# Conv on eight small tiles from a shifted copy, eight output buffers and a regrouped start, in a Conv + low-rank mixer kernel

## The chip, the cores and the metric

The kernel runs on one core of one Trainium2 chip. The metric is the device time of one execution in microseconds (us). Before the change the median of 8 runs is 340.77 us (338.88 to 341.13). A core has a matrix engine (TensorE, in the profile PE for its matmuls and PEld for its weight loads), a vector engine (DVE), an activation engine (ACT), GpSimd (POOL) and SyncE (SP). The last two only start DMA transfers here, apart from some set-up work on POOL. Matmul results go to PSUM[...]; DVE or ACT must copy ("evacuate") them to SBUF.

## What is computed

```python
# x: [8, 4224, 192], weight: [8 heads, 7 taps], U: [4224, 32], V: [32, 4224]
w = softmax(weight, axis=-1)
y[b, s, head h] = sum over k of w[h, k] * x_pad[b, s + k, head h]   # causal, 6 zero rows ahead
h = (y.transpose(0, 2, 1) @ U @ V).transpose(0, 2, 1)
u = y + h
out = u + maximum(u @ w_ch1, 0) @ w_ch2          # w_ch1: [192, 768], w_ch2: [768, 192]
```

The first line of work is called Conv below, the second the low-rank sum, and the two matrix products of the last line W1 and W2.

## The kernel before

*Layout.* The sequence of a batch is cut into 66 blocks of 64 rows. An x tile has 128 partitions: the lower 64 hold blocks 0 to 31 with an empty block ahead, the upper 64 hold blocks 31 to 65, the first again as the halo. It is loaded from HBM in four parts (XP, L83) by POOL, which also turns f32 into bf16. x tiles come from a pool of three (xs, L46).

*Conv* (L297). One call does some heads of one batch. The weights are a band matrix per head. Each output of 64 rows takes two matmuls: one with the block itself, one with the block ahead of it (halo), accumulated in PSUM. Both have 64 input rows and 64 output rows[...]. For one head of batches 1 to 7 these are eight matmuls of 384 or 408 columns into two banks; row half r writes bank r. ACT evacuates one bank, DVE the other (L272, L274).

*Low-rank sum.* tt_mm (L334) multiplies the Conv result by U, 33 small matmuls (L340). tt_split (L350) splits it in a high and a low half, tt_sum (L393) adds four row groups, and tt_done copies the sum to SBUF (L390). h_group (L456, called "h" in the plan) then makes u for a group of eight 128-row tiles: small matmuls (L425), and DVE additions that write u (L447).

*The mixer.* SP transposes u by DMA (L466) into uT; w1 (L511) does 36 matmuls of 512 columns (L519), whose results ACT and DVE pass through a ReLU (L530, L532); w2 (L537) does 12 matmuls of 192 columns per two tiles (L543), DVE adds u (L551) into one of four output buffers (outs, L51), and SP stores it (L558). 33 groups in all.

*Order.* The program order of each engine is written out by hand. SLOTS (L571) lists, per slot, the groups for w1, the groups for w2, the Conv heads between them, and at which w2 piece other steps stand: h (with the transpose of that group), t (tt_mm and tt_split) and s (tt_sum). From slot 5 on a slot has three groups: w1 of three groups, then Conv, then 12 w2 pieces with the other steps between them. The x parts of a later batch are started by POOL, each held until a given block of w1 has run (LOADS, L607, and held, L611). DMAs of one queue are issued in program order, so a transfer that waits holds up those behind it.

*Start.* Batch 0 is loaded and convolved in three pieces (KP, L85; x_piece, L87). While the weights of the Conv are being built, PE runs matmuls on zeros (idle, L170): 60 of 128 columns, then three and two of 512 columns around the first piece. The first two groups get their transposes from PE (L477, L492).

Of the kernel before, what the change touches and what calls it, by code (L numbers as in the profile page):

```python
# [9 lines left out]
BF16 = mybir.dt.bfloat16  # L10
# [4 lines left out]
def kernel(  # L15
# [10 lines left out]
    nc = tc.nc  # L26
    P = nc.NUM_PARTITIONS
    B, S, D = x.shape
    H, KC = weight.shape
    GS = D // H  # L30
    R = moe_U.shape[1]
    M4 = moe_w_ch1.shape[1]
    NT = S // P
# [6 lines left out]
    HB = P // 2  # L40
    QB = 32
# [1 line left out]
    ctx.enter_context(tc.manual_schedule())  # L43

    cst = ctx.enter_context(tc.tile_pool(name="cst", bufs=1))
    xs = ctx.enter_context(tc.tile_pool(name="xs", bufs=3))  # L46
    ys = ctx.enter_context(tc.tile_pool(name="ys", bufs=3))
    us = ctx.enter_context(tc.tile_pool(name="us", bufs=7))
    uts = ctx.enter_context(tc.tile_pool(name="uts", bufs=5))
    rls = ctx.enter_context(tc.tile_pool(name="rls", bufs=3))  # L50
    outs = ctx.enter_context(tc.tile_pool(name="outs", bufs=4))  # L51
    sml = ctx.enter_context(tc.tile_pool(name="sml", bufs=2))
    psp = ctx.enter_context(tc.tile_pool(name="psp", bufs=8, space=bass.MemoryType.PSUM))

    def bank():
        return psp.tile([P, 512], F32, name="ps", tag="ps")
# [4 lines left out]
    xt = [None] * B  # L61
    yt = [None] * B
# [3 lines left out]
    NB0 = 32  # L66
    NB1 = S // HB - NB0
# [14 lines left out]

    XP = [(0, 1, 17), (0, 17, NB0 + 1), (1, 0, 18), (1, 18, NB1 + 1)]  # L83

    KP = [(0, 7), (7, 13), (13, NB1 // 2)]  # L85

    def x_piece(k):  # L87
        for r in range(2):
            k0, k1 = KP[k]
            k1 = min(k1, (NB0, NB1)[r] // 2)  # L90
            x_part(0, r, (1 - r if k == 0 else 2 * k0 + 1), 2 * k1 + 1)
# [25 lines left out]

    fp = cst.tile([P, P], I32, name="fp")
    nc.gpsimd.iota(fp[:], pattern=[[1, P]], base=P, channel_multiplier=-1)
    x_piece(1)  # L120

    efp = cst.tile([P, 4, P], I32, name="efp")
    nc.gpsimd.iota(efp[:], pattern=[[-1, 4], [1, P]], base=4 * P, channel_multiplier=-4)
# [8 lines left out]
    )  # L132
    nlast = NT * 32 - nfull * P
    nc.gpsimd.dma_start(out=Ur[0:nlast, nfull, :], in_=U4[nfull * P :, :])
    x_piece(2)


    V0_sb = cst.tile([32, 2 * GT * P], BF16, name="V0_sb")
# [31 lines left out]
    def idle(n, w):  # L170
        wps = bank()
        for _ in range(n):
            nc.tensor.matmul(  # L173
                out=wps[:, 0:w], lhsT=zz[:, 0:P], rhs=zz[:, 0:w], start=True, stop=True
            )
# [94 lines left out]
    def evac(eng, out, in_):  # L270
        if eng == "A":
            nc.scalar.activation(out=out, in_=in_, func=ACT.Copy)  # L272
        else:
            nc.vector.tensor_copy(out=out, in_=in_)  # L274
# [19 lines left out]
            )  # L294


    def conv(b, h0, nh, rs, engs, k0=0, k1=NT):  # L297

        if yt[b] is None:
            yt[b] = ys.tile([P, NT, D], BF16, name="y_sb")  # L300
        nk = {r: min(k1, (NB0, NB1)[r] // 2) - k0 for r in rs}
        pp = {r: bank() for r in rs}
        w = nh * GS
        for hh in range(nh):
            h = h0 + hh
            for halo in range(2):
                for r in rs:
                    for c in range(2):
                        st = 1 - halo + c + 2 * k0
                        nc.tensor.matmul(  # L310
                            out=pp[r][HB * c : HB * c + HB, 0 : nk[r] * w].rearrange(
                                "p (k a) -> p k a", a=w
                            )[:, :, hh * GS : hh * GS + GS],
                            lhsT=band[HB * r : HB * r + HB, h, HB * halo : HB * halo + HB],
                            rhs=xt[b][
                                HB * r : HB * r + HB,
                                st : st + 2 * nk[r] - 1 : 2,
                                h * GS : h * GS + GS,
                            ],
                            start=(halo == 0),  # L320
                            stop=(halo == 1),
                            tile_position=(HB * r, HB * c),
                        )
        for n, r in enumerate(rs):
            j0 = NB0 // 2 * r + k0
            evac(
                engs[n % len(engs)],
                yt[b][:, j0 : j0 + nk[r], h0 * GS : h0 * GS + w],
                pp[r][:, 0 : nk[r] * w].rearrange("p (k a) -> p k a", a=w),
            )  # L330
# [55 lines left out]
            )  # L386

    def tt_done(b, p):
        t = sml.tile([P, D], BF16, name="tt_sb")
        nc.vector.tensor_copy(out=t[:], in_=p[:, 0:D])  # L390
        ttb[b] = t

# [71 lines left out]
    def transp(g):  # L464
        uTt[g] = uts.tile([P, 4, 3, P], BF16, name="uT")
        nc.sync.dma_start_transpose(  # L466
            out=uTt[g][:].rearrange("p i c t -> p (i c) t"),
            in_=ut[g][:].rearrange("p i c f k -> p (i c f k)"),
        )
# [90 lines left out]
    def held(ins, after):  # L560
        tc.add_manual_dep(
            ins.ins,
            after.ins.name,
            mybir.DependencyInfo(mybir.DependencyClass.Sync, mybir.DependencyReason.DATA),
            reason="load held back",
        )
# [2 lines left out]


    SLOTS = [  # L571
        ([0], [], [], {}),
        ([1], [0], [], {0: ["h0"], 1: ["h3"]}),
        ([2], [1], [(1, 0, 8)], {0: ["h1"], 1: ["t1"], 3: ["s1"], 4: ["h4"]}),
        ([3], [2], [(2, 0, 4)], {1: ["h5"]}),
        (
            [4, 5],
            [3, 4, 5],
            [(2, 4, 8)],
            {1: ["t2", "h6"], 3: ["s2"], 4: ["h7"], 7: ["h8"], 10: ["h9"]},  # L580
        ),
    ]
    CONV = {
        5: [(3, 0, 8)],
        6: [(4, 0, 8)],
        7: [(5, 0, 4)],
        8: [(5, 4, 8), (6, 0, 3)],
        9: [(6, 3, 8), (7, 0, 2)],
        10: [(7, 2, 8)],
    }  # L590
    SUMS = {5: (3, 5), 6: (4, 10), 8: (5, 2), 9: (6, 6), 10: (7, 10)}
    nh = 10
    for k in range(5, 14):
        gs = list(range(3 * k - 9, 3 * k - 6))
        at = {}
        for p in (1, 5, 9) if k == 5 else (2, 6, 10):
            if nh < NG:
                at.setdefault(p, []).append(f"h{nh}")
                nh += 1
        if k in SUMS:  # L600
            b, p = SUMS[k]
            at.setdefault(p, []).insert(0, f"t{b}")
            at.setdefault(p + 2, []).insert(0, f"s{b}")
        SLOTS.append((gs, gs, CONV.get(k, []), at))
    assert nh == NG

    LOADS = {2: [(1, 5), (1, 5), (2, 2), (2, 5)]}  # L607
    for b, g in ((3, 4), (4, 6), (5, 9), (6, 12), (7, 15)):
        LOADS[b] = [(g, 1), (g, 4), (g + 1, 1), (g + 1, 4)]

    def held(ins, after):  # L611
        tc.add_manual_dep(
            ins.ins,
            after.ins.name,
            mybir.DependencyInfo(mybir.DependencyClass.Sync, mybir.DependencyReason.DATA),
            reason="load held back",
        )


    idle(3, 512)  # L620
    for h in range(0, H, 2):
        conv(0, h, 2, [0, 1], "AD", *KP[0])
    idle(2, 512)
    for h in range(0, H, 2):
        conv(0, h, 2, [0, 1], "AD", *KP[1])
    u_layout()
    yT = yT_part(0)
    jb = NB0 // 2
    rest = [(KP[2][0], jb), (jb + KP[2][0], NT)]
    ps0 = bank()  # L630
    U4_sb, tf = tt_first(
        ps0, list(range(KP[2][0])) + list(range(jb, jb + KP[2][0])), rest
    )
    for h in range(0, H, 4):
        conv(0, h, 4, [0, 1], "AD", *KP[2])
    nc.tensor.matmul(out=ps0[:, 0:D], lhsT=R4f[:], rhs=tf[:], start=True, stop=False)  # L636
    tt_more(ps0, U4_sb, rest)
    tt_done(0, ps0)
# [4 lines left out]
        x_part(1, *xp)  # L643

    def do(what):
        n = int(what[1:])
        if what[0] == "h":
            h_group(n)
            if n > 1:
                transp(n)  # L650
        elif what[0] == "t":
            tt_split(n, tt_mm(n, range(NT)))
        else:
            tt_sum(n)

    for gs1, gs2, convs, at in SLOTS:
        for g in gs1:
            ends = w1(g, RELU0 if g < 2 else RELU)
            for b, blocks in LOADS.items():
                for q, (gb, m) in enumerate(blocks):  # L660
                    if gb == g:
                        if q == 0:
                            x_tile(b)
                            x_zero(b, nc.gpsimd)
                        held(x_part(b, *XP[q]), ends[m])
            if g == 0:
                hT_part(1, yT_part(1), "AD")
                do("h2")
        n = sum(h1 - h0 for _, h0, h1 in convs)
        for b, h0, h1 in convs:  # L670
            for h in range(h0, h1):
                conv(b, h, 1, [0, 1], "AD" if n > 2 else "A")
        npc = 4 * len(gs2)
        for p in range(npc + 1):
            for what in at.get(p, []):
                do(what)
            if p < npc:
                g, k = gs2[p // 4], p % 4
                if g == NG - 1 and k == 3:
                    w2(g, 6, 1)  # L680
                    w2(g, 7, 1)
                else:
                    w2(g, 2 * k, 2)
# [30 lines left out]
```

## Time and profile before

| | |
|---|---|
| median of 8 runs | 340.77 us |
| the profiled execution | 340.99 us |
| its span | 339.2 us |
| mean granted PE clock | 0.993 |
| DMA traffic | 53.55 MB, mean 158 GB/s |
| DMA queue of SP | 38.18 MB, 45.2% of 16 engines |
| DMA queue of POOL | 14.73 MB, 37.4% |
| landing of a store of 192 KB, median | 2.8 us |
| landing of a part of x, median | 7.5 to 9.1 us |
| landing of a transpose, median | 4.0 us |

Busy time of an engine is the union of its instructions. Matmuls are pipelined and their ends are modelled, so PE can be busy and still not run at its peak; distances between the starts of two groups of matmuls are the safer measure. In lines of groups, "x133 | 70.1, 551" means 133 instructions, 70.1 us busy together, 551 ns each; behind the second bar stands the idle time of the engine just before them and what ended most of it. In timelines the columns are the start, the duration from the first to the last instruction of the merged group, engine, line and operation. In the chain of waits they are start, duration and instruction. A store's or a load's landing time is counted from its issue to the last byte.

### The profile page before, as it was taken

The numbers are of one execution on the slowest core, as the hardware profiler recorded it, in microseconds if no ns is written. First come the engines' busy times: TensorE is split into PE (matmuls) and PEld (weight loads), VectorE is DVE, ScalarE is ACT, GpSimd is POOL, SyncE is SP. The second block draws the span as 40 slices with busy tenths as digits, with TensorE's granted clock in tenths as the row PEclk, the third lists the DMA queues.
The fourth block names the chain that finished last, engine by engine and source line by source line (L and its number), as shares of the span: only waits on it lengthen the run. The fifth ranks groups of instructions, "written<-read, shape, count | busy, mean of one in ns | idle before, by whom it ended". The sixth has DMA issues, their size and how long they took to land.

```text
span 339.2 us, 9771 instructions
## 1 busy us (share of the span) xinstructions
PE 327.1 (96%) x4111; PEld 231.4 (68%) x4111; DVE 280.4 (83%) x571; ACT 160.4 (47%) x327; POOL 39.3 (12%) x65
## 2 busy tenths in 40 slices
PE   8789999999999999999999999999999998999995
PEld 7555675678557856965974884696587487487595
DVE  5736999988888888988898889889898887886863
ACT  1648446550492097059039308704912911922910
POOL 8660210120120040012012000000000000000000
PEclk9979999999999999999999999999999999999999
DMA  9999995699996999799799696069049238429135
GB/s 107 192 167 135 167 209 130 126 193 255 183 207 103 223 195 134 197 192 204 123 277 183 108 230 146 2 186 234 2 112 243 69 90 237 96 72 254 48 118 165
DMA packets 122941, 53.55 MB, mean 158 GB/s; under 512 B 87792, under 2 KB 122864, under 8 KB 122896
## 3 DMA queue, kind: packets, MB, share of 16 engines
q1 hardware_dynamic: 84672, 38.18, 45.2%
q0 software_dynamic: 38224, 14.73, 37.4%
q8 instruction: 32, 0.52, 0.6%
q14 instruction: 13, 0.11, 0.1%
HBM read 29.49 MB, written 25.95 MB: 163 GB/s over the span
## 4 chain that ended last, share of the span: by engine, by line
PE 77%; DVE 8%; DMA 8%; ACT 3%; issue 2%; POOL 1%; DVEq 0%; POOLq 0%
PE ps L519 35%; PE ps L543 30%; DMA out_dram<-out_sb 8%; PE ps L310 7%; DVE out_sb L551 3%; ACT rl_sb L530 2%; PE ps L340 2%; DVE u_sb L447 2%; PE ps L425 2%; DVE y_sb L274 1%; DVE pr L223 1%; DVE rl_sb L532 1%; POOL x_sb L78 1%; PE ps L173 0%; PE ps L636 0%
## 5 line engine op out<-in xcount | busy, mean ns | idle before, releaser
L530 ACT ACTIVATE rl_sb<-ps 128x512 bf16<-128x512 f32 x235 | 126.0, 604 | 108.5 <-PE ps L519 87.0
L543 PE MATMUL ps<-W_sb,rl_sb 128*128 128x192 bf16 x1584 | 139.1, 246 | 1.8 <-DVE out_sb L551 1.7
L543 PEld LDWEIGHTS <-rl_sb 128*128 128x128 bf16 x1584 | 128.9, 98 | 10.7 <-issue 10.4
L519 PE MATMUL ps<-uT,W_sb 64*128 64x512 bf16 x1188 | 133.5, 376 | 1.7 <-DVE uT L274 0.8
L532 DVE TENSOR_SCALAR rl_sb<-ps 128x512 bf16<-128x512 f32 x161 | 104.0, 688 | 15.3 <-PE ps L519 14.9
L519 PEld LDWEIGHTS <-W_sb 64*128 64x128 bf16 x1188 | 61.4, 94 | 69.5 <-issue 7.2
L551 DVE TENSOR_TENSOR out_sb<-ps,u_sb 128x384 f32<-128x384 f32 (+1 forms) x133 | 70.1, 551 | 25.9 <-DMA out_dram<-out_sb 12.8
L447 DVE TENSOR_TENSOR u_sb<-y_sb,ps 128x192 bf16<-128x192 bf16 (+1 forms) x168 | 66.2, 461 | 0.0
L78 POOL DMA_DIRECT2D x_sb<-in_x_dram x34 | 28.1, 834 | 140.3 <-PE ps L519 126.2
L274 DVE CAST y_sb<-ps 128x408 bf16<-128x408 f32 (+3 forms) x66 | 32.6, 560 | 3.7 <-PE ps L310 3.5
L310 PE MATMUL ps<-x_sb,band 64*64 64x384 bf16 (+5 forms) x640 | 27.2, 305 | 0.0
L272 ACT ACTIVATE y_sb<-ps 128x384 bf16<-128x384 f32 (+2 forms) x66 | 26.1, 509 | 1.0 <-PE ps L310 0.9
L310 PEld LDWEIGHTS <-band 64*64 64x64 bf16 x640 | 18.8, 111 | 9.2 <-issue 7.3
L354 ACT ACTIVATE tt_hi<-ps 128x192 bf16<-128x192 f32 x7 | 2.3, 331 | 41.1 <-PE ps L340 41.1
L425 PE MATMUL ps<-tt_sb,V_sb 32*128 32x192 bf16 x264 | 12.1, 246 | 0.2 <-DVE y_sb L274 0.2
L425 PEld LDWEIGHTS <-V_sb 32*128 32x128 bf16 x264 | 4.6, 92 | 6.3 <-issue 6.0
L173 PE MATMUL ps<-zz 128*128 128x128 bf16 (+1 forms) x65 | 7.6, 308 | 1.2 <-DVE zz L168 1.2
L340 PE MATMUL ps<-y_sb,U_sb 128*32 128x192 bf16 x257 | 7.6, 255 | 0.0
L173 PEld LDWEIGHTS <-zz 128*128 128x128 bf16 x65 | 6.4, 141 | 1.4 <-DVE zz L168 1.2
L340 PEld LDWEIGHTS <-U_sb 128*32 128x32 bf16 x257 | 5.6, 98 | 1.2 <-issue 1.1
L355 DVE TENSOR_TENSOR tt_lo<-ps,tt_hi 128x192 bf16<-128x192 f32 x7 | 2.5, 356 | 3.6 <-ACT tt_hi L354 3.6
L240 ACT ACTIVATE band<-ps 32x152 bf16<-32x152 f32 x8 | 2.3, 288 | 3.2 <-PE ps L231 3.1
(57 smaller groups left out, 46.9 us busy)
## 6 DMA issues: line engine op xcount, KB each, us to landing
out_dram<-out_sb SPq DMA_DIRECT2D x131, 192.0 KB, 2.8
x_sb<-in_x_dram POOLq DMA_DIRECT2D x14, 384.0 KB, 7.5
x_sb<-in_x_dram POOLq DMA_DIRECT2D x7, 432.0 KB, 9.1
x_sb<-in_x_dram POOLq DMA_DIRECT2D x7, 408.0 KB, 9.0
x_sb<-in_x_dram POOLq DMA_DIRECT2D x2, 288.0 KB, 5.9
uT<-u_sb SPq DMA_TRANSPOSE x31, 4.0
W_sb<-in_moe_w_ch_dram POOLq DMA_DIRECT2D x2, 192.0 KB, 6.1
x_sb<-in_x_dram POOLq DMA_DIRECT2D x1, 360.0 KB, 6.1
```

The lines of the kernel that those rows point to most:

```text
L78: return nc.gpsimd.dma_start(out=xt[b][HB * r : HB * r + HB, s0:s1, :], in_=x[b, blk * HB : (blk + s1 - s0) * HB, :].rearrange("(j p) d -> ...
L272: nc.scalar.activation(out=out, in_=in_, func=ACT.Copy)
L274: nc.vector.tensor_copy(out=out, in_=in_)
L310: nc.tensor.matmul(out=pp[r][HB * c : HB * c + HB, 0 : nk[r] * w].rearrange("p (k a) -> p k a", a=w)[:, :, hh * GS : hh * GS + GS], lhsT=b ...
L340: nc.tensor.matmul(out=p[32 * c : 32 * c + 32, o : o + D], lhsT=U_sb[:, j // 4, j % 4, :], rhs=yt[b][:, j, :], start=(n < 4), stop=(n + 4 ...
L425: nc.tensor.matmul(out=banks[pr][:, a * D : (a + 1) * D], lhsT=V_sb[32 * q : 32 * q + 32, (j // 8) * 2 + j % 2, :], rhs=ttb[b][32 * q : 32 ...
L447: nc.vector.tensor_tensor(out=u_group(g)[:, i : i + n, :, hf, :], in0=yt[b][:, run[0] : run[0] + n, :].rearrange("p n (c k) -> p n c k", c=3),
L519: last = nc.tensor.matmul(out=pp[hf][:], lhsT=W1_sb[HB * hf : HB * hf + HB, c, m * P : (m + 1) * P], rhs=uTt[g][HB * hf : HB * hf + HB, :, ...
L530: nc.scalar.activation(out=rl[:, m, hf, :], in_=pp[hf][:], func=ACT.Relu)
L532: nc.vector.tensor_scalar_max(out=rl[:, m, hf, :], in0=pp[hf][:], scalar1=0.0)
L543: nc.tensor.matmul(out=cps[:, a * D : (a + 1) * D], lhsT=rlt[g][:, m, hf, (i + a) * P : (i + a + 1) * P], rhs=W2_sb[:, m, :], start=(m == ...
L551: nc.vector.tensor_tensor(out=o[:, 0:n, :].rearrange("p n (c k) -> p n c k", c=3), in0=cps[:, 0 : n * D].rearrange("p (n c k) -> p n c k", ...
```

## The change

Four things are changed.

- The pool of output buffers has eight buffers instead of four. The pool of x tiles has two instead of three, and a new pool xbs has one tile for the shifted copy.
- Batch 0 comes in two pieces (blocks for 13 output columns, then the rest) instead of three. The second of the new pieces is issued where the third was. Its Conv of the first piece runs head by head.
- The idle matmuls of 512 columns are replaced by 30 of 128 columns behind the band's matmuls.
- Conv of batches 1 to 7 is done by conv32. Each output has only 32 rows, so that 64 input rows contain its halo, and one matmul is enough. Half of the outputs need their input moved by 32 rows; x_shift makes this copy with four DMAs from SBUF to SBUF on the SP queue. Tiles are 64 rows by 32 columns, eight at a time. The Conv steps ("c") and the copies ("x") now stand in the slot plan between w2 pieces, mostly in groups of two or three heads at pieces 0, 1 and 2, and the places of h, t and s move with them.

The edits, cut to their core:

```diff
-    xs = ctx.enter_context(tc.tile_pool(name="xs", bufs=3))
+    xs = ctx.enter_context(tc.tile_pool(name="xs", bufs=2))
+    xbs = ctx.enter_context(tc.tile_pool(name="xbs", bufs=1))
-    outs = ctx.enter_context(tc.tile_pool(name="outs", bufs=4))
+    outs = ctx.enter_context(tc.tile_pool(name="outs", bufs=8))
-    KP = [(0, 7), (7, 13), (13, NB1 // 2)]
+    KP = [(0, 13), (13, NB1 // 2)]
...
+    def x_shift(b):
+        xbt[b] = xbs.tile([P, NB1, D], BF16, name="xb_sb")
+        q = [slice(QB * r, QB * r + QB) for r in range(4)]
+        for dst, src, n in ((2, 1, NB0), (0, 3, NB1)):
+            nc.sync.dma_start(out=xbt[b][q[dst], 0:n, :], in_=xt[b][q[src], 0:n, :])
+            nc.sync.dma_start(out=xbt[b][q[dst + 1], 0:n, :], in_=xt[b][q[src - 1], 1 : n + 1, :])
+
+    def conv32(b, h0, nh, engs):
+        if yt[b] is None:
+            yt[b] = ys.tile([P, NT, D], BF16, name="y_sb")
+        nk = (NB0 // 2, NB1 // 2)
+        for n in range(nh):
+            h = h0 + n
+            hs = slice(h * GS, h * GS + GS)
+            pp = [bank(), bank()]
+            for c in range(2):
+                for src in range(2):
+                    for r in range(2):
+                        t, o, cg = ((xt[b], 1, 2 * c + 1), (xbt[b], 0, 2 * c))[src]
+                        part = (r, 1 - r)[src]
+                        st = o + c
+                        nc.tensor.matmul(
+                            out=pp[part][QB * cg : QB * cg + QB, 0 : nk[part] * GS],
+                            lhsT=band[HB * r : HB * r + HB, h, QB : 2 * QB],
+                            rhs=t[HB * r : HB * r + HB, st : st + 2 * nk[part] - 1 : 2, hs],
+                            start=True,
+                            stop=True,
+                            tile_position=(HB * r, QB * cg),
+                        )
+            for part in range(2):
+                j0 = NB0 // 2 * part
+                evac(engs[(2 * n + part) % len(engs)], ...)
...
     SLOTS = [
-        ([1], [0], [], {0: ["h0"], 1: ["h3"]}),
-        ([2], [1], [(1, 0, 8)], {0: ["h1"], 1: ["t1"], 3: ["s1"], 4: ["h4"]}),
-        ([3], [2], [(2, 0, 4)], {1: ["h5"]}),
-        ([4, 5], [3, 4, 5], [(2, 4, 8)],
-            {1: ["t2", "h6"], 3: ["s2"], 4: ["h7"], 7: ["h8"], 10: ["h9"]}),
+        ([1], [0], {0: ["h0"], 1: ["h3", "x1"]}),
+        ([2], [1], {0: ["c1:0:3:AAD", "h1"], 1: ["c1:3:3:AD"], 2: ["c1:6:2:AD"],
+                    3: ["t1"], 4: ["s1", "h4", "x2"]}),
+        ([3], [2], {1: ["h5"]}),
+        ([4, 5], [3, 4, 5],
+            {0: ["c2:0:2:AAD"], 1: ["c2:2:3:AD", "h6"], 2: ["c2:5:3:AD"],
+             4: ["t2", "h7"], 6: ["s2"], 7: ["h8"], 10: ["h9"], 12: ["x3"]}),
...
     for k in range(5, 14):
+        if k == 5:
+            hp = (6, 9, 11)
+            put(0, "c3:0:3:AD")
+            put(2, "c3:3:3:A")
+            put(7, "c3:6:2:AAD")
+            put(11, "s3")
+        elif k < 10:
+            hp = (5, 8, 11)
+            put(0, f"c{k - 2}:0:2:AAD")
+            put(1, f"c{k - 2}:2:3:AD")
+            put(2, f"c{k - 2}:5:3:AD")
+            put(8, f"s{k - 2}")
+        else:
+            hp = (0, 4, 8)
...
+        if k < 10:
+            put(hp[k == 5], f"t{k - 2}")
+        if k < 9:
+            put(12, f"x{k - 1}")
...
-    idle(3, 512)
-    for h in range(0, H, 2):
-        conv(0, h, 2, [0, 1], "AD", *KP[0])
-    idle(2, 512)
-    for h in range(0, H, 2):
-        conv(0, h, 2, [0, 1], "AD", *KP[1])
+    idle(30, P)
+    for h in range(H):
+        conv(0, h, 1, [0, 1], "AD", *KP[0])
```

The loads of x (LOADS) keep their places.

## The prediction

> **What bounds the kernel now.** I read four views in this order: the busy times of the engines, the chain of waits, the groups of instructions, and then the timelines of TensorE (PE) and of the SP queue, slot by slot.
>
> ```profile
> PE 327.1 (96%) x4111; PEld 231.4 (68%) x4111; DVE 280.4 (83%) x571; ACT 160.4 (47%) x327; POOL 39.3 (12%) x65
> ...
> PE 77%; DVE 8%; DMA 8%; ACT 3%; issue 2%; POOL 1%; DVEq 0%; POOLq 0%
> ```
> PE is the bound. The 19% of the chain on DVE, DMA and ACT says that it is made to wait in places. The groups say where from:
>
> ```profile
> L551 DVE TENSOR_TENSOR out_sb<-ps,u_sb 128x384 f32<-128x384 f32 (+1 forms) x133 | 70.1, 551 | 25.9 <-DMA out_dram<-out_sb 12.8
> L310 PE MATMUL ps<-x_sb,band 64*64 64x384 bf16 (+5 forms) x640 | 27.2, 305 | 0.0
> ```
> DVE stood 12.8 us before its output additions because all four output buffers were still being stored. The Conv (L310) holds PE for 27.2 us; the PE timeline shows the pieces:
>
> ```profile
> 117.80 12.34 PE L519 MATMUL ps<-uT,W_sb 64*128 64x512 bf16 x108
> 130.07 3.34 PE L310 MATMUL ps<-x_sb,band 64*64 64x384 bf16 x64
> ...
> 159.56 1.57 PE L310 MATMUL ps<-x_sb,band 64*64 64x384 bf16 x32
> ...
> 174.28 11.83 PE L519 MATMUL ps<-uT,W_sb 64*128 64x512 bf16 x108
> ```
> Here the reader takes the distance from one start to the next. A slot's first layer (W1, 108 matmuls) takes 11.76 us undisturbed (174.28 to 186.04) and 12.27 us in the slot at 117.80. The Conv takes 3.28 us for eight heads and 1.51 us for four. Added over batches 1 to 7 this is 3.30+1.51+1.51+3.28+3.28+1.51+2.81+2.82+2.33 = 22.35 us. From the chain I read the price of changing the tiling:
>
> ```profile
> 133.41 2.09 PE ps L543 x24
> 135.50 0.28 PE ps L425 x8
> 135.78 4.07 PE ps L543 x48
> ```
> 24 more matmuls of the second layer cost 4.07-2.09 = 1.98 us, 82.5 ns each, so 0.11 us of either piece is the change of tile shape. A visit to another shape costs about 0.2 us, there and back.
>
> [...] the 64-partition x loads do run at a flat 190 GB/s or so, but they read twice these bytes from HBM.[...]
>
> **The change, part by part**, against the profiled execution (340.99 us, span 339.2; 0.2 us above the median of 340.77).
>
> 1. *Conv of batches 1 to 7 on PE.* 448 matmuls stay 448, each now with its own output and eight tiles at once instead of four. Nearest row: 33 matmuls with 32 weight columns (L340) in 0.85 us, 25.8 ns each, four tiles of 192 columns. Eight tiles of some 396 columns stream almost the same per matmul, so 448 x 25.8 ns = 11.6 us. Visits: each batch is now spread over three, the first 0.1 us (PE changes shape after W1 anyway), the others 0.2 us: 7 x 0.5 = 3.5 us. Sum 15.1 for 22.35: **-7.3 us**; bounds -8.5[...] and +1 (no more overlap than before, below). The 16 evacuations per batch and their sizes stay; DVE does seven or fewer of them instead of up to eight.
>
> 2. *Eight output buffers.* The PE losses behind this wait, from its timeline: 0.40 at 82.36, 0.30 at 87.24, 1.30 in W1 from 87.24 (13.06 for 11.76), 0.5 in W1 at 117.80, 0.3 at 147.49, 0.21 at 201.32, 1.08 at 284.38, 0.53 in the last W1. Sum 4.6. DVE is late from its own work in some of them: I take **-4.0 us**; bounds -4.6 and -2.5.
>
> 3. *Start.* The first two loads are almost twice as long; POOL's issue of one is 0.69 us for 6 or 8 blocks and 0.87 for 18, so the two add about 0.2 us ahead of the iotas and the band. 53 blocks land as one: 1.30 MB at 190 GB/s from about 4 us, near 11 us, where the second piece stood before. The 30 idle matmuls (55 ns each, estimated as 128/192 of the 82.5 ns above) follow the band's at 9.7 and end near 11.3, so Conv runs at about 11.4 to 14 and its evacuations (16 of 0.47 us on two engines) to 15.5. The old kernel stood until 16.05 in an unexplained wait (1.98 us at "issue"), and its clock was 0.5 from 17 to 20.7. If the idle matmuls keep the clock, up to 1.3 us is won; the rest is hidden. **-0.8 us**; bounds -2.5 and +1.
>
> 4. *The shift, new.* Each batch sends 4 DMAs of 393 to 406 KB from SBUF to SBUF on the SP queue, 1.6 MB together, 11.2 MB in all on top of 53.55. The second matmul pair of the first head needs them: the upper and the lower half each wait for two, so PE stands until all four have landed, and behind it stand all evacuations and second-layer work. Batch 1 is the tight one. Its shift stands in SP's queue behind the transpose of group 3:
>
> ```profile
> 38.54 2.40 SPq L466 DMA_TRANSPOSE uT<-u_sb  x1
> 40.98 11.70 SPq L558 DMA_DIRECT2D out_dram<-out_sb  x7
> ```
> So it issues at 41.0. Estimate for landing: 2.0 us of fixed time (the shortest store landed in 2.0 in this part of the trace)[...]: 50.3. PE wants it at 42.4. The wait is 7.9 us less 0.4 that PE lost there before: **+7.5 us**; at 380 GB/s (the read rate of the x loads) it is 4.2 us of data and +4.4; with the loads of batch 2 in the way, up to +10. The stores queued behind the shift have free buffers and nobody waits for them.
>
> For batches 3 to 6 the shift is queued at the end of a slot, behind the transpose and one store. SP reaches a transpose 2.8 us after its h matmuls (171.91 to 174.69); h now stands before the last second-layer piece, 1.4 us before the next W1 starts, so transpose at +1.4, store at +2.9, shift at +3.3, landing at +12.6[...], without other traffic. The Conv wants it at +11.8. But the loads of the next x batch go out in the same W1 (119.61, 122.02, 123.97 and 125.91 in the slot of 117.80) and fill the DMA engines:
>
> ```profile
> 126.00:128.00 2.00, 2.00 (x22) 1.03 (x18) 2.00 (x4) 1.90 (x4) 0.97 (x2) 1.00 1.55 203
> 128.00:130.00 2.00, 2.00 (x20) 0.89 (x15) 1.40 (x3) 1.96 (x5) 0.00 (x0) 1.00 1.60 197
> 130.00:132.00 2.00, 2.00 (x47) 1.66 (x50) 2.00 (x5) 1.97 (x6) 0.00 (x0) 1.00 1.61 188
> ```
> (last two columns: DMA share, GB/s.) I add 0.9 us for sharing: a wait of 1.7 us in each of four slots, 0.8 in the slot of batch 7, which has no loads: **+7.6 us**; bounds 0 (shift at over 250 GB/s) and +16. Batch 2 has a whole slot of cover: nothing. Its x tile is free in time with two buffers instead of three: the Conv two batches before ends a slot earlier.
>
> 5. *Moved work.* In the slot of groups 4 and 5, DVE now has 7 Conv copies (0.5), 12 outputs (0.51), 4 h groups (2.07) and 0.7 of sums after W1: 18.6 us against 17.0 for PE, with group 6's additions in the midst of the Conv's banks. Its lag is taken up in the next W1, where DVE has 2.4 us to spare: +1.4. In the next slot the sum of batch 3 and group 12, which needs it, stand side by side: matmul, DVE copy (0.35), matmul, with nothing between: +0.8. Elsewhere DVE has 16.1 us beside 15.8 of PE in the second part of a slot, and W1 absorbs it. **+2.2 us**, bounds +0.5 and +4. DVE becomes the next bound in these stretches; that is why no further gain may be booked.
>
> Sum: -7.3 -4.0 -0.8 +7.5 +7.6 +2.2 = +5.2: **346 us**.
>
> **Rivals.**
> *The shift lands in time* (the other side). One mechanism: the data rate of the four DMAs. From 1.6 MB in 6.5 us, 246 GB/s, upward, nothing waits in the later slots. For it: stores over 128 partitions reach 374 GB/s in a slice of the DMA view, and the packets are long (12 KB). Against: [...]the loads. Then part 4 is +4.4 and 0: -7.3-4.0-0.8+4.4+2.2 = -5.5, **335.5 us**.
> *The eight tiles don't overlap.* In a head both row halves write the same bank at once, in different quarters. If this makes them take turns, the Conv stays at 44 to 47 ns per matmul, about 20 us with 3.5 of visits: part 1 becomes +1, with the forecast's shift waits, partly hidden by the longer Conv, **353 us**. Against: the quarters are disjoint.
> *The shift is starved by the loads.* [...]if the shift gets half of the engines, it lands at +16, waits of 4 us in four slots: part 4 at 17+8, **355 us**; I count it as the upper end of the forecast.
>
> **How the numbers follow.** The forecast holds 0.55 (own range 341.5 to 354, its high end the starved shift), in time 0.31 (333 to 340), no overlap 0.14 (346 to 358). About 0.3% is what a measurement of this kernel tells from no change. Faster: nearly all of the in-time case, 0.31; same: 0.07 from the seam of the two cases; slower: 0.62. The range 334.5 to 354 leaves out the upper part of the no-overlap case and the lower tail.
>
> **What would show it.** Part 1: heads at 0.2 us each on the PE timeline. Part 2: no DVE wait on the store. Part 4: PE idle before Conv, released by the shift's DMA, near 42 to 50 us and at the ends of W1 in the slots from 90 us on; the landing time of these DMAs, 9 us or more. If they land in 6 us or less, the forecast is wrong and the second case holds; if the Conv matmuls of a head still take 0.37 us, the third does.

## The result, and the profile after

The changed kernel takes 402.87 us (median of 11 runs, 397.74 to 403.44) against 340.57 us for the kernel before on the same chips: a ratio of 1.180, 95% interval 1.177 to 1.183. It is 62 us slower. The forecast was 346 us, range 334.5 to 354: the sign was right, the size was not. The profiled execution has a span of 396.0 us and a mean granted PE clock of 0.922 (before 339.2 and 0.993).

First the page of the changed kernel: the busy times, the granted clock, and the shares of the chain of waits.

```profile
PE 332.4 (84%) x4072; PEld 223.7 (56%) x4072; DVE 276.8 (70%) x561; ACT 165.8 (42%) x337; POOL 37.9 (10%) x63
...
PEclk9999759958998599969967997899999999999999
...
PE 59%; DMA 23%; DVE 10%; SPq 4%; issue 2%; ACT 2%; POOL 0%; DVEq 0%; POOLq 0%
```

PE's share of the chain fell from 77% to 59%, DMA's rose from 8% to 23%. PE is no longer the bound for the first 70% of the span: its clock row dips below 9 again and again there. The groups of instructions on the same page say who is waited for:

```profile
L562 PE MATMUL ps<-uT,W_sb 64*128 64x512 bf16 x1188 | 133.8, 381 | 11.5 <-DMA uT<-u_sb 10.7
...
L594 DVE TENSOR_TENSOR out_sb<-ps,u_sb 128x384 f32<-128x384 f32 (+1 forms) x133 | 70.5, 549 | 27.3 <-PE ps L586 26.7
...
L324 PE MATMUL ps<-xb_sb,band 64*32 64x384 bf16 (+1 forms) x224 | 17.8, 414 | 43.6 <-DMA xb_sb<-x_sb 43.6
```

The new Conv (L324) made PE stand 43.6 us for its shift copies. The first layer (L562) stood 10.7 us for one transpose of u, a wait that the kernel before did not have. The additions to the output (L594) no longer wait for stores: that part of the change did what it says. PE's timeline shows what each wait drags behind it (start, first to last instruction, engine, line; in brackets the idle time before):

```profile
53.30 0.52 PE L324 MATMUL ps<-xb_sb,band 64*32 64x408 bf16 x2 [12.39 <-DMA xb_sb<-x_sb]
...
87.51 6.50 PE L562 MATMUL ps<-uT,W_sb 64*128 64x512 bf16 x36 [10.73 <-DMA uT<-u_sb]
93.94 0.34 PE L324 MATMUL ps<-x_sb,band 64*32 64x384 bf16 x2
...
94.41 1.17 PE L586 MATMUL ps<-W_sb,rl_sb 128*128 128x192 bf16 x12
95.50 0.35 PE L324 MATMUL ps<-x_sb,band 64*32 64x384 bf16 x2
...
96.14 1.00 PE L468 MATMUL ps<-tt_sb,V_sb 32*128 32x192 bf16 x8
...
112.28 11.83 PE L562 MATMUL ps<-uT,W_sb 64*128 64x512 bf16 x108
...
131.75 0.52 PE L324 MATMUL ps<-xb_sb,band 64*32 64x408 bf16 x2 [7.36 <-DMA xb_sb<-x_sb]
...
132.89 4.02 PE L586 MATMUL ps<-W_sb,rl_sb 128*128 128x192 bf16 x24
```

At full clock two heads of the Conv take 0.47 us (93.94 to 94.41) and three 0.64 (95.50 to 96.14), so the eight tiles do overlap. But the Conv of batch 3 begins at 131.75, 7.4 us late, and the 24 second-layer matmuls behind it take 4.02 us instead of 2.0: the granted clock has fallen to 0.50 while PE stood. The view of stretches shows it; its columns are the stretch and its length, busy times of PE, PEld, DVE, ACT and POOL, and last the granted clock, the DMA share and GB/s:

```profile
128.00:130.00 2.00, 0.00 (x0) 0.00 (x0) 0.00 (x0) 0.00 (x0) 0.00 (x0) 0.50 0.96 178
...
132.00:134.00 2.00, 2.00 (x30) 1.24 (x15) 1.56 (x3) 1.25 (x3) 0.00 (x0) 0.50 1.98 182
```

The 36 first-layer matmuls at 87.51 take 6.50 us for some 3.9. Over 40 to 280 us, in slices of 2 us, I multiplied PE's busy time by what the clock lacked: 14.5 us are lost in this way.

SyncE's queue for batch 1 shows when the copies are issued:

```profile
36.74 2.01 SPq L509 DMA_TRANSPOSE uT<-u_sb  x1
38.88 0.61 SPq L305 DMA_DIRECT2D xb_sb<-x_sb  x1
39.54 0.58 SPq L306 DMA_DIRECT2D xb_sb<-x_sb  x1
40.22 1.94 SPq L305 DMA_DIRECT2D xb_sb<-x_sb  x1
42.20 1.95 SPq L306 DMA_DIRECT2D xb_sb<-x_sb  x1
```

The first goes out at 38.9, the last at 42.2, and the Conv gets its data at 53.3. In batches 3 to 6 it is some 15 us from the first issue to the last landing; in batch 7, with no loads of x beside it, 9.9 us.

What I had not read is in the view of stretches of the kernel *before* (columns as above):

```profile
40.00:200.00 160.00, 158.57 (x2012) 111.70 (x2007) 140.68 (x286) 78.36 (x159) 19.41 (x27) 1.00 1.02 182
200.00:330.00 130.00, 128.57 (x1502) 89.86 (x1500) 109.74 (x217) 62.10 (x120) 0.00 (x0) 1.00 0.50 130
```

From 40 to 200 us, the stage in which the x batches are loaded, the DMA engines were at a share of 1.02 (in this view it can pass 1, as the 1.55 to 1.61 of the prediction do) already, moving 182 GB/s; after 200 us at 0.50. The copies are 11.35 MB (64.90 less 53.55 in all), those of six batches of seven beside loads. At 182 GB/s they need 62 us, about the size of the loss. That is arithmetic, not a proof; the experiments test it. The changed kernel moved less in the same stretch, not more:

```profile
40.00:200.00 160.00, 121.75 (x1468) 76.39 (x1464) 102.43 (x209) 64.35 (x130) 14.97 (x21) 0.86 1.02 174
```

### The profile page after: what moved, and what is told of

It reads as the page before. It is cut to its first block, busy times and chain, and to the rows that moved or that the text cites. A ratio compares the mean times of both kernels' runs of the same rounds, so it can differ in the third digit from the quotient of the medians.

```text
span 396.0 us, 9752 instructions
## 1 busy us (share of the span) xinstructions
PE 332.4 (84%) x4072; PEld 223.7 (56%) x4072; DVE 276.8 (70%) x561; ACT 165.8 (42%) x337; POOL 37.9 (10%) x63
## 2 busy tenths in 40 slices
DMA packets 124253, 64.90 MB, mean 164 GB/s; under 512 B 88208, under 2 KB 123280, under 8 KB 123312
## 3 DMA queue, kind: packets, MB, share of 16 engines
q0 software_dynamic: 38192, 14.73, 36.3%
## 4 chain that ended last, share of the span: by engine, by line
PE 59%; DMA 23%; DVE 10%; SPq 4%; issue 2%; ACT 2%; POOL 0%; DVEq 0%; POOLq 0%
PE ps L586 32%; PE ps L562 18%; DMA xb_sb<-x_sb 17%; PE ps L324 4%; DVE u_sb L490 3%; DMA uT<-u_sb 3%; SPq L305 3%; DMA x_sb<-in_x_dram 2%; DVE out_sb L594 2%; DVE rl_sb L575 2%; PE ps L468 2%; PE ps L383 2%; ACT rl_sb L573 1%; SPq L306 1%; DVE y_sb L274 1%
## 5 line engine op out<-in xcount | busy, mean ns | idle before, releaser
L586 PE MATMUL ps<-W_sb,rl_sb 128*128 128x192 bf16 x1584 | 146.5, 253 | 0.1
L562 PE MATMUL ps<-uT,W_sb 64*128 64x512 bf16 x1188 | 133.8, 381 | 11.5 <-DMA uT<-u_sb 10.7
L586 PEld LDWEIGHTS <-rl_sb 128*128 128x128 bf16 x1584 | 133.3, 100 | 15.6 <-issue 14.7
L562 PEld LDWEIGHTS <-W_sb 64*128 64x128 bf16 x1188 | 58.3, 95 | 82.7 <-DMA uT<-u_sb 11.2
L594 DVE TENSOR_TENSOR out_sb<-ps,u_sb 128x384 f32<-128x384 f32 (+1 forms) x133 | 70.5, 549 | 27.3 <-PE ps L586 26.7
L274 DVE CAST y_sb<-ps 128x408 bf16<-128x408 f32 (+2 forms) x56 | 28.3, 557 | 48.2 <-PE ps L324 45.7
L272 ACT ACTIVATE y_sb<-ps 128x384 bf16<-128x384 f32 (+3 forms) x76 | 31.4, 491 | 67.3 <-PE ps L324 65.6
L324 PE MATMUL ps<-xb_sb,band 64*32 64x384 bf16 (+1 forms) x224 | 17.8, 414 | 43.6 <-DMA xb_sb<-x_sb 43.6
L324 PEld LDWEIGHTS <-band 64*32 64x32 bf16 x448 | 5.9, 98 | 52.8 <-DMA xb_sb<-x_sb 43.2
L324 PE MATMUL ps<-x_sb,band 64*32 64x384 bf16 (+1 forms) x224 | 20.2, 405 | 0.1
L468 PE MATMUL ps<-tt_sb,V_sb 32*128 32x192 bf16 x264 | 13.9, 249 | 1.4 <-DVE tt_sb L433 1.3
L173 PE MATMUL ps<-zz 128*128 128x128 bf16 x90 | 8.2, 278 | 1.2 <-DVE zz L168 1.2
```

Source lines behind the costliest of these rows:

```text
L324: nc.tensor.matmul(out=pp[part][QB * cg : QB * cg + QB, 0 : nk[part] * GS], lhsT=band[HB * r : HB * r + HB, h, QB : 2 * QB], rhs=t[HB * r ...
L468: nc.tensor.matmul(out=banks[pr][:, a * D : (a + 1) * D], lhsT=V_sb[32 * q : 32 * q + 32, (j // 8) * 2 + j % 2, :], rhs=ttb[b][32 * q : 32 ...
L562: last = nc.tensor.matmul(out=pp[hf][:], lhsT=W1_sb[HB * hf : HB * hf + HB, c, m * P : (m + 1) * P], rhs=uTt[g][HB * hf : HB * hf + HB, :, ...
L586: nc.tensor.matmul(out=cps[:, a * D : (a + 1) * D], lhsT=rlt[g][:, m, hf, (i + a) * P : (i + a + 1) * P], rhs=W2_sb[:, m, :], start=(m == ...
L594: nc.vector.tensor_tensor(out=o[:, 0:n, :].rearrange("p n (c k) -> p n c k", c=3), in0=cps[:, 0 : n * D].rearrange("p (n c k) -> p n c k", ...
```

## Experiments

The theory at first was that the copies land late, and that their own landing (four transfers over 32 partitions each) sets the waits. The rivals were their place in the queue, their width of 32 partitions, and the loads beside them.

**1. No copies, and copies that nobody reads.** In both kernels the shifted half of the Conv reads the unshifted tile, so half of the Conv's outputs are of other rows.

```diff
-                        t, o, cg = ((xt[b], 1, 2 * c + 1), (xbt[b], 0, 2 * c))[src]
+                        t, o, cg = ((xt[b], 1, 2 * c + 1), (xt[b], 0, 2 * c))[src]
-                        st = o + c
+                        st = (o + c, 0)[src]
```

The first also has no x_shift. Expected:

> The changed kernel without the four copies; the matmuls that read the shifted tile read the x tile itself, same sizes, so half of the Conv's outputs are of other rows. Theory 'late copies' (the loss is the wait for the copies and what follows from it): the forecast's other parts remain, -7.3 -4.0 -0.8 +2.2, that is about 331 us, 330 with the start as measured; no wait of PE over 1 us, the clock stays full. Rival 'the new Conv or the new order is slow in itself': 345 us or more.

> The four copies are issued as in the changed kernel, but nobody reads them: the Conv reads the x tile itself (half of its outputs are of other rows). 'Late copies': nearly all of the loss goes; what stays is the transpose that stands behind the copies in SP's queue (10.7 us of PE), so 335 to 347 us. Rival 'the traffic of the copies slows the whole kernel': 370 us or more.

Measured: 329.82 us (ratio 0.968, interval 0.964 to 0.973) and, in two runs, 363.57 us (1.067, 1.056 to 1.079). The first is as expected: without the copies everything else in the change, two x tiles instead of three included, is worth 11 us, and the granted clock is 1.00. Copies that nobody waits for still cost 34 us, between the two expectations for the second: neither held. The waits had moved to the transposes of u (16.2 us). So the copies harm others, not only the Conv. In this kernel the stretch from 40 to 200 us moved 200 GB/s, so the 182 of the kernel before were no ceiling.

**2. Copies earlier.** Batch 1's ahead of h0, those of batches 3 to 7 at piece 8 of the slot instead of 12.

```diff
-        ([1], [0], {0: ["h0"], 1: ["h3", "x1"]}),
+        ([1], [0], {0: ["x1", "h0"], 1: ["h3"]}),
-            put(12, f"x{k - 1}")
+            put(8, f"x{k - 1}")
```

> The copies of batches 3 to 7 are issued at piece 8 of a slot instead of 12, those of batch 1 ahead of the transpose of group 3. 'Late copies': the waits of batches 3 to 7 (31 of 43.6 us) fall to 0 to 1 us each and batch 1's from 12.4 to about 6; the wait for the transpose of group 5 stays: 345 to 360 us. Rival 'the copies are too slow for any place' (the waits only move): 385 us or more.

Measured: 388.06 us (1.139, 1.129 to 1.148). PE's waits in this kernel (what waited, for what: sum, times, longest):

```profile
PE ps L562 <- DMA uT<-u_sb: 36.3, 4, 12.2
...
PE ps L324 <- DMA xb_sb<-x_sb: 7.2, 2, 6.0
```

The Conv's wait fell from 43.6 to 7.2 us, as meant. In its place the first layer waits 36.3 us for transposes, which now stand behind the copies. In batches 3 to 6 the copies go out 5.5 to 8 us earlier against the first layer of their slot; most of that is paid back one step later. The time is that of the rival, whose sign was that the waits only move.

**3. Is it the queue?** The changed kernel and the one with early copies, now with the copies issued by GpSimd (`nc.gpsimd.dma_start` in x_shift), so that transposes and stores no longer stand behind them.

> The changed kernel with one edit: the four shift copies of each batch are issued by GpSimd instead of SyncE, at the same places of the program; what is computed is unchanged. New theory, queue order: a copy's bytes stand in SyncE's queue in front of the transposes of u and the stores, and a transpose issued behind them lands late (12.9 us instead of 4.1 for group 5). Then the 10.7 us wait for uT goes, the Conv's waits for its copies (43.6 us in all) stay or shrink by one or two us each because the copies no longer stand behind h3's transpose: 380 to 394 us. Rival, all queues share engines that are full: the transposes are late just the same, 398 to 405 us.

> The kernel of the earlier run with copies issued earlier (at piece 8 of their slots), and the copies issued by GpSimd instead of SyncE; what is computed is unchanged. There the Conv had stopped waiting for copies (7.2 us left), and the transposes of u waited 36.3 us in the copies' place. Queue order: with the copies in another queue the transposes land in 5 us or so, neither wait is left but batch 1's, and the time is 340 to 355 us. Rival, full engines: the transposes' waits stay at over 20 us, 370 to 390 us.

Measured: 391.66 us for the first (four runs, 379.7 to 395.6, too wide for an interval) and 383.97 us for the second (1.126, 1.118 to 1.134). The first lies in the range of the queue theory, but by luck: in its profile PE waits 36.0 us for transposes and 8.5 for copies, the reverse of what the theory said. In the second, in a profile of the longest of its runs (394.2 us), PE's wait for transposes and the landing times are (size and median us from issue):

```profile
PE ps L562 <- DMA uT<-u_sb: 35.0, 8, 10.4
...
xb_sb<-x_sb POOLq DMA_DIRECT2D x14, 408.0 KB, 10.4
...
uT<-u_sb SPq DMA_TRANSPOSE x31, 9.6
```

The transposes, alone with the stores in their queue, now land in 9.6 us at the median, against 4.1 without copies, and PE still waits 35.0 us for them. The other three runs (379.5 to 384.7 us) have no profile, but they too are some 40 us above the kernel before, where the queue theory wanted 355 at most. The order in SyncE's queue alone falls as the cause.

**4. Is it the width or the lump?** One kernel copies nearly the same bytes (3% more) over all 128 partitions, unshifted (half of the Conv's outputs are of other rows). Another, with early copies on SyncE, cuts each copy of batches 3 to 7 into thirds, one behind each transpose of the slot.

```diff
+        for a, z, o in ((0, 9, 0), (9, 17, 0), (17, 25, 0), (25, 34, 1)):
+            nc.sync.dma_start(out=xbt[b][:, a:z, :], in_=xt[b][:, a - o : z - o, :])
```

```diff
-            put(8, f"x{k - 1}")
+            for i, p in enumerate(hp):
+                put(p, f"x{k - 1}:{i}")
```

> The same bytes as in the changed kernel (1.6 MB per batch in four DMAs at the same places), but each over all 128 partitions and unshifted, so half of the Conv's outputs are of other rows. [...]the copies of batch 7, which have no loads beside them, land about 6 us after the first issue instead of 9.9, and the time falls to 375 to 392 us. If the rate is bound elsewhere (DMA engines, loads of x), landing and time stay: 398 to 405 us.

> The kernel of the earlier run with copies issued earlier, SyncE's queue again, but the copies of batches 3 to 7 are cut into thirds of their blocks, each third issued right behind one of the slot's three transposes, so that about 3 us of copy stand in front of the next transpose 6 us later instead of 10 to 15; [...]what is computed is unchanged. [...]batches 3 to 7 stop waiting, for copies and for transposes alike, and only batches 1 and 2 wait: 345 to 360 us. Rival, the total of bytes on the DMA engines is too much for a slot: the waits turn up again at some place of each slot, 370 us or more.

Measured: wide copies 369.4 and 375.9 us (two runs, no interval), thirds 379.23 us (1.115, 1.109 to 1.122). Width is worth some 30 of the 73 us that the copies cost, more than expected. The copies of batch 7, with no loads beside them, show it most plainly: in four narrow DMAs they took 9.9 us, wide they had landed within 6.9 us of the first issue (249.10; PE went on at 256.00 without a wait). The wide copies also have shorter packets, 3 KB or so instead of 12 (3,616 packets from 2 to 8 KB, against 32 with narrow copies); that this alone helped is not likely, since experiment 7 finds no gain in shorter packets. But some 43 us stay with all 128 partitions in use, though this kernel moves more:

```profile
40.00:200.00 160.00, 129.76 (x1663) 84.36 (x1658) 111.77 (x228) 69.65 (x143) 16.00 (x23) 0.91 1.05 198
```

Spreading the lump is worth 9 us; the waits turn up elsewhere (21.0 us for copies, 17.3 for transposes).

**5. The loads of x taken away.** Batches 2 to 7 are not loaded; their Conv and copies read the tiles of batches 0 and 1, so all that depends on these batches' x is of other data. Once with early copies, once with the copies where the change has them.

```diff
-                            x_tile(b)
-                            x_zero(b, nc.gpsimd)
-                        held(x_part(b, *XP[q]), ends[m])
+                            xt[b] = xt[b % 2]
```

> The kernel with copies issued earlier, all copies on SyncE as before, but the loads of x for batches 2 to 7 left out: their Conv and their copies read the tiles of batches 0 and 1 again, so Conv, sums and outputs of batches 2 to 7 are computed from other batches' x; every instruction but the loads is there. Newest theory, full DMA engines: in the stage with loads of x the engines are full already without copies (a share of 0.96 to 1.08 in each 40 us from 40 to 200 us of the kernel before), so copies and whatever shares the engines are late by the work added; without the loads the copies fit, the transposes land in 5 us again: 333 to 346 us, most of it over 330 being batch 1. Rival, the copies themselves[...] make the waits: 365 to 388 us.

> The changed kernel with its copies where they are, and only the loads of x for batches 2 to 7 left out (Conv, sums and outputs of these batches are computed from the tiles of batches 0 and 1). Contention: of the 73 us that the changed kernel takes over the kernel without copies (402.9 against 329.8) most goes; what stays is copies that land in 8 to 10 us where the Conv wants them after 7, waits of 2 to 3 us in batches 3 to 7 with a cold clock behind, and batch 1: 345 to 362 us. Rival, landing behind the transposes at the slot's end is late by itself: 375 us or more.

Measured: 344.26 us (1.009, 1.006 to 1.013) and 363.27 us (1.066, 1.061 to 1.072). In the first, every copy is still there, and:

```profile
40.00:200.00 160.00, 149.09 (x1959) 96.03 (x1956) 132.62 (x268) 83.46 (x171) 0.00 (x0) 0.98 0.73 169
```

```profile
uT<-u_sb SPq DMA_TRANSPOSE x31, 4.1
```

(stretch as above with its DMA share of 0.73; landing of the transposes, 4.1 us again). Removing the loads brings 44 us where the copies are early. In the kernel without copies PE waits only 0.6 us for a load. And no copy waits for the data of a load: SyncE's queue has no such wait, neither in the changed kernel nor in the one with early copies. So it is the traffic of copies and loads together that is shown to be the main cause there; 14 us over the kernel without copies stay. In the change's own order it brings 40 of the 73 us, a little less than expected; the other 33 are 10.4 of cold clock (worked out as above) and these waits:

```profile
PE ps L324 <- DMA xb_sb<-x_sb: 18.4, 6, 7.6
PE ps L562 <- DMA uT<-u_sb: 3.7, 1, 3.7
```

**6. Half of the copies.** Two of the four copies of each batch left out, early order; half of the shifted matmuls read the unshifted tile, so a quarter of the Conv is of other rows.

```diff
-        for dst, src, n in ((2, 1, NB0), (0, 3, NB1)):
+        for dst, src, n in ((0, 3, NB1),):
```

> The kernel with copies issued earlier, with two of the four copies of each batch left out (5.7 MB instead of 11.4), and half of the shifted matmuls reading the unshifted tile, so a quarter of the Conv is of other rows; the same matmuls. Full DMA engines: the excess over the kernel without copies (329.8 us against 388.1 with all) falls by more than half, because the part that fits in between is free: 335 to 358 us. Rival, waits set by the landing of one copy[...]: 370 to 388 us.

Measured: 355.58 us (1.040, 1.035 to 1.044). The excess over no copies is 25.8 us, where all of them cost 58.2: a bit less than half for half the bytes. The cost goes with the amount that is copied; since bytes and number of copies are halved together, this run does not tell which of the two.

**7. Is it the packets?** First the loads of batches 2 to 7 in packets of some 6 KB instead of 384 bytes (the same bytes to the same partitions, rows in another order), then the copies in packets of 1,536 and of 384 bytes instead of 12 KB; all with early copies.

```diff
-            in_=x[b, blk * HB : (blk + s1 - s0) * HB, :].rearrange("(j p) d -> p j d", p=HB),
+            in_=x[b, blk * HB : (blk + s1 - s0) * HB, :].rearrange(
+                "(j p) d -> p j d" if b < 2 else "(p j) d -> p j d", p=HB
+            ),
```

```diff
+                for par in range(2):
+                    f = xbt[b][q[d], 0:32, :].rearrange("p (c t k) d -> p c t (k d)", t=2, k=K)
+                    g = xt[b][q[s], o : o + 32, :].rearrange("p (c t k) d -> p c t (k d)", t=2, k=K)
+                    nc.sync.dma_start(out=f[:, :, par, :], in_=g[:, :, par, :])
```

> The kernel with copies issued earlier; the loads of x for batches 2 to 7 bring the same bytes to the same partitions, but each partition's blocks from one contiguous stretch of HBM, packets of some 6 KB instead of 384 bytes, so the rows of x in these batches stand in another order. If the DMA engines are full because of the loads' short packets, the loads leave room and the time comes near that without loads (344.3 us): 340 to 355 us. Rival, the bytes[...] are what is short: it stays near 388 us, 375 or more.

> The kernel with copies issued earlier, the loads of x as in the change, but each copy cut so that its packets are 1,536 bytes (four blocks of one partition) instead of 12 KB: two DMAs of every other group of four blocks in place of one, and one more for the last two blocks of the longer copies, ten DMAs a batch instead of four; same bytes, [...]what is computed is unchanged. Theory, long packets hold up what shares the engines with them, the transposes above all: these land in 5 to 6 us again and the time is 340 to 365 us. Rival, bytes[...]: it stays at 380 us or more.

> As the run with packets of 1,536 bytes, with packets of 384 bytes (single blocks). Theory of long packets: the transposes are in time here too, unless so many short packets take more of the engines than the long ones, which is then seen in SyncE's share of them: 340 to 370 us. Rival, bytes[...]: 380 us or more.

Measured: 435.54 us (1.277, 1.268 to 1.286), 393.90 us (1.157, 1.152 to 1.162) and 408.34 us (1.202, 1.196 to 1.207), against 388.06 with early copies alone. None of the three packet lengths gives the time back. The last two are as the rival said, and their ten DMAs a batch instead of four also mean more issuing by SyncE. The first is a surprise, outside of both expectations: fewer packets, and slower by 47 us, with this wait on the transposes:

```profile
PE ps L564 <- DMA uT<-u_sb: 82.7, 6, 25.8
```

Why long load packets hold the transposes up so much is open.

**8. The shift without DMAs.** GpSimd copies the tiles of batches 2 to 7 itself, from piece 4 of the slot (batch 4 from piece 8, where the expectation says batch 3); batch 1 keeps its DMAs.

```diff
+        copy = nc.sync.dma_start if b == 1 else nc.gpsimd.tensor_copy
+            copy(out=xbt[b][q[dst], 0:n, :], in_=xt[b][q[src], 0:n, :])
```

> The shift made by GpSimd's own copies (four of 32 partitions by 6,144 to 6,528 elements for each batch, issued from piece 4 of the slot, batch 3 from piece 8) instead of DMAs, for batches 2 to 7; batch 1 keeps its DMAs, issued ahead of h0; what is computed is unchanged. Full DMA engines: the transposes and loads are as in the kernel without copies; GpSimd's rate isn't in the profile, its iota of 512 elements took 0.57 us, so some 7 us a copy and 28 a batch, in time for the next slot; batch 1 waits 6 us and runs cold behind it: 334 to 348 us. Rival, GpSimd is half as fast or slows VectorE: each Conv waits over 10 us, 390 us or more.

Measured: 352.86 us (1.031, 1.026 to 1.036), 50 us better than the change, yet 5 us past the range expected and still 12 worse than before. A copy takes 5.46 us:

```profile
L307 POOL COPY xb_sb<-x_sb 32x6144 bf16<-32x6144 bf16 (+1 forms) x12 | 65.5, 5460 | 0.5
```

PE waits 8.0 us for GpSimd's copies and 4.8 for batch 1's DMAs. Part of the lateness is GpSimd's own order: its copies wait 21.2 us for loads that it issues itself, behind the copies of the batch ahead. The cold clock takes 5.6 us (worked out as above). The last 4 or 5 us over the kernel without copies I did not trace.

**9. The parts that gain, alone.** The kernel before with eight output buffers, and that with the new start too.

```diff
-    outs = ctx.enter_context(tc.tile_pool(name="outs", bufs=4))
+    outs = ctx.enter_context(tc.tile_pool(name="outs", bufs=8))
```

```diff
-    KP = [(0, 7), (7, 13), (13, NB1 // 2)]
+    KP = [(0, 13), (13, NB1 // 2)]
...
-    idle(3, 512)
+    idle(30, P)
```

> The kernel before with eight output buffers instead of four and nothing else. The prediction's term: the wait on stores goes and 4.0 us with it (bounds 2.5 to 4.6): 336 to 338.3 us. Rival, the next thing is late by as much: 340 to 341 us.

> The kernel before with its own Conv, eight output buffers and the new start (batch 0 in two pieces, the idle matmuls, one head a visit); what is computed is unchanged. The start brought the first group's matmuls 1.8 us forward in the changed kernel, and eight buffers alone gave 335.2 us: 332.5 to 334.5 us. Rival, the start's gain is eaten by a later wait (transposes, first weights): 335 to 337 us.

Measured: 335.18 us (0.988, 0.983 to 0.992) and 334.46 us (0.981, 0.978 to 0.984). Both beat the kernel before, and the second is the fastest of those that leave no work out. The chain of waits of the kernel with eight buffers has lost its DMA share:

```profile
PE 92%; DVE 3%; ACT 2%; issue 1%; POOL 1%; POOLq 0%; DVEq 0%
```

The new start is worth 0.7 us by the medians, more by the ratios, whose intervals overlap: what it adds is not separated from nothing.

## Why the prediction was wrong, by its steps

*Step 1, Conv on PE, -7.3 us: right in kind, a bit small.* Eight tiles overlap. In the kernel without copies, where nothing stops PE, the 21 visits of batches 1 to 7 take 13.6 us with the changes of shape (0.47 us for two heads and 0.64 for three in most), where I had 15.1: -8.8 us, just past my bound of -8.5. The rival without overlap is out. That two row halves write one bank at once in different quarters costs nothing that shows here: the 16 matmuls of two heads are done in 0.47 us, 29 ns each, where the case without overlap had 44 to 47.

*Step 2, eight buffers, -4.0 us: right.* Alone they give 4.0 us by the medians (1.25% with the interval above: 2.6 to 5.9).

*Step 3, the start, -0.8 us: not contradicted.* The clock held (1.00 granted from 11 to 21.1 us, where the kernel before had 0.50 from 18 to 20), and the first group's first layer began at 21.10 instead of 22.90 us. But with eight buffers and the old start it began at 21.21 in its profile, so this trace can't say that the start brought it.

*Step 5, moved work, +2.2 us: not measured alone.* Steps 1, 2, 3 and 5 together were put at -9.9 us. The kernel without copies has them all and measured -10.9 by the ratio. The forecast's error is not there.

*Step 4, the shift, +15.1 us together: this is the step that failed.* It cost 73 us (402.9 less 329.8). Its terms, against the trace:

- "Batch 2 has a whole slot of cover: nothing." The Conv did not wait, but the copies did not come free. The transpose of group 5, issued behind them, landed in 12.9 us instead of 4.1, and PE stood 10.7 us. I asked only who waits for the copies, not who is late because of them.
- Batch 1: wait of 7.9 us predicted, 12.4 measured, 2 us past what I had allowed for loads in the way (+10).
- Batches 3 to 7: "1.7 us in each of four slots", 0.8 in batch 7. Measured 7.4, 5.8, 8.1, 7.5 and 2.5: 31.2 us, with batch 1 43.6. In batches 3 and 4 the copies left 4.9 and 3.4 us after the start of the first layer, near the 3.3 that I had, but landed some 15 us later and not 9.3 or 10.2. In batch 7, without loads beside them, they took 9.9 us: the 9.3 that I had without other traffic, an estimate of mine that no row of the trace showed, was near, and what failed is the 0.9 us for the loads, which cost some 5.
- Nothing was booked for the clock behind a wait: 14.5 us. PE of the kernel before had hardly stood, so no row priced it, but the clock of 0.5 in the start, which I quoted, was the warning.

These are 43.6 + 10.7 + 14.5 = 68.8 of the 73 us. Below them lies one mistake. I quoted a DMA share of 1.55 to 1.61 in a slot, and priced it as "0.9 us for sharing". Read over the stage, 182 GB/s at a share of 1.02, it should have warned me: at that rate 1.62 MB more for each batch is 8.9 us of DMA for every slot of 27 to 30 us. Asking only where the copies land hid this. It is a warning and not a price, though: the same bytes cost 34 us when nobody reads them, some 43 when they are wide, 49 in thirds, 58 when early and 73 as changed. My upper bound of +16 for batches 3 to 7 was passed by the Conv's waits alone (31.2 us).

The rival with the shift starved by the loads (355 us) had the mechanism, with a landing of 12.7 us from issue, and it too counted only the Conv. What is shown: the copies cost the 73 us (experiment 1), and much of it goes with the loads of x beside them (5), with the amount that is copied (6) and with the width of the copies (4). Another queue (3) and other packets (7) do not give it back. What stays open is what the copies and loads run short of, in the DMA engines or at the memory on either side: the kernels with copies and loads moved 170 to 200 GB/s from 40 to 200 us at shares of 0.98 to 1.20, and no run tells these apart. Of the 33 us that the change's own order costs even without loads, 19 go when the copies are issued earlier (363.27 against 344.26 us): issued last in the slot, behind the transposes, those of batch 4 take 9.6 us to land (139.1 to 148.7), and the Conv wants them after 8.5.

## What to carry to other kernels

Before a change adds DMA traffic, read the DMA share and GB/s of the stage where it will run, not of the whole span: where the share is near 1, expect a cost of the order of the new bytes over that stage's rate (62 us here, 34 to 73 measured), whoever ends up waiting. When a wait is moved by issuing a transfer earlier, look at what then stands beside it; here the wait went from the Conv to the transposes at four fifths of the price (58 of 73 us). And price a wait of PE with the cold clock that follows: a quarter again in this kernel (14.5 us on 54.3), nearly half in the one without loads (10.4 on 22.1).

## What was not expected of the hardware

- The DMA transposes suffered most from other traffic when GpSimd issued the early copies. Without copies they landed in 4.1 us at the median; there in 9.6, where stores went from 2.8 to 3.7 us and the larger parts of x from 9.5 and 10.1 to 13.9 and 15.9. With copies in SyncE's queue and loads in 6 KB packets one took 36.6 us.
- Longer packets for the loads lowered the load queue's share of the engines only from 33.2% of 387 us to 26.9% of 432 us (128 to 116 us of all engines), with 14,000 packets instead of 38,192.
- The issue of one copy holds SyncE's queue for 0.5 to 2.2 us.
- GpSimd copies 32 partitions of 6,144 to 6,528 bf16 in 5.46 us, 0.86 ns an element, beside a busy VectorE whose additions to the output took 552 ns there and 549 ns in the changed kernel.
